# Moving one of three integer additions per score group, and most normalisations, from VectorE to GpSimd

## The chip, the core and the metric

The kernel runs on one core of a Trainium2 chip. The core's engines run side by side, each through its own list of instructions in order: TensorE (PE in the profile) multiplies matrices into PSUM, ScalarE (ACT) applies functions, VectorE (DVE) and GpSimd (POOL) do elementwise work, and SyncE (SP) issues most DMA transfers. An instruction can wait for a semaphore that another engine's instruction raises. The metric is the time of one execution in microseconds (us); lower is better.

## What is computed

Two independent layers share one launch. Part A is attention with 32 query heads and one key and value head. Part B is linear attention, in which queries and keys become two softmaxes of 16 features each.

```python
q = (x @ wq).reshape(B, S, H, Dh)...; k = x @ wk; v = x @ wv          # A: S=2048, H=32, Dh=16
p = softmax(einsum("bhqd,bkd->bhqk", q, k) * Dh**-0.5)
a = einsum("bhqk,bkd->bhqd", p, v)... @ wo
...
phi_k = concat([softmax(k @ w_phi), softmax(-k @ w_phi)])             # B, and phi_q in the same way
kv = einsum("bhsf,bhsd->bhfd", phi_k, v); z = sum over s of phi_k
b = (phi_q @ kv) / (phi_q @ z + 1e-6) @ wo
return concat([a, b], axis=-1)
```

Part A has 32 x 2048 x 2048 exponentials, which is 2048 score tiles of 128 keys by 512 columns. They are most of the work.

## The kernel before, in words

**Two ways to an exponential.** The 2048 score tiles are handled in groups of four (a "quad"): four tiles that share 128 keys and go to one accumulation. 388 of the 512 quads take the ScalarE way. TensorE computes scores in batches of three and two tiles (line 1617, job `qk`), ScalarE exponentiates a batch in one instruction (line 1678, job `ex`, into the ring `PT`), and TensorE multiplies four finished tiles with the values (line 1732, job `pv`, 4 matmuls). The other 124 quads take the VectorE way. TensorE computes one tile at a time (job `dq`, also line 1617), and VectorE turns it into 16-bit integers whose bits, read as a float16, are roughly the exponential (line 1788, job `dz`, into row 0 of the buffer `Z`). When all four tiles of the quad are there, VectorE makes three more versions of them, each the first plus a constant, 256 times 1, 2 and 3 (line 1801, job `dS`, into rows 1 to 3 of `Z`). TensorE then multiplies all four versions with four differently scaled copies of the values and adds them up (line 1834, job `dpv`, 16 matmuls). Their weighted sum is a better exponential than one version alone. `Z` has three buffers (`NQ = 3`).

**After 16 quads** one of the 32 accumulations (`sc`) is complete. VectorE copies it out of PSUM (`ac`, to `accS`), takes the reciprocal of the denominators (`rc`, line 1866), which small DMAs on SyncE gather and spread, and multiplies the two (`on`, line 1884, to `On` or `Od`). The results of eight accumulations feed the output projection of A.

**Part B** is threaded through the first 420 us or so: projections on TensorE, exponentials on ScalarE (lines 2058 and 2148), row sums, reciprocals and products on VectorE. GpSimd sets up constants at the start and does one small step in the middle of B (`kvfin`, lines 2126 to 2131). It does nothing else.

**What sets the order.** A planner in the kernel writes every engine's instruction list ahead of time. Each piece of work is a job with an engine, an assumed duration, a priority and the jobs it needs. The planner keeps a clock for each engine, and always issues the job that can start first by its own assumed durations; among those that could start together the priority decides, with a small random term whose seed changes every 20 us of the plan (`SEEDS`). ScalarE's next score batch has the highest priority on TensorE. The `dq` jobs use what is left of TensorE and VectorE, limited by `dbusy`, an account of VectorE's pending work, so the split between the two ways is an outcome of the plan: a quad that goes to VectorE is one that ScalarE never sees. Where TensorE would otherwise stand idle too long, the planner adds dummy matmuls (`fill` and `company`, lines 1424 and 1407). At run time only semaphores count: each instruction waits for those it depends on, and an engine never goes past a waiting instruction.

Of the kernel before, what the change touches and what calls it, by code (L numbers as in the profile page):

```python
# [7 lines left out]
ALU = mybir.AluOpType  # L8
# [1162 lines left out]
class _Fast:  # L1171
# [16 lines left out]
    def __init__(self, nc, st, ins, out):  # L1188
# [33 lines left out]
        self.ones = sb("ones", [128, 128], BF)  # L1222
        self.zero = sb("zero", [128, 128], BF)
# [41 lines left out]
        self.spq = 30.0  # L1265

# [5 lines left out]
    def add(self, eng, fn, reads=(), writes=(), accum=(), **k):  # L1272
        if self.rec is not None:
            self.rec.append((eng, tuple(reads), tuple(writes) + tuple(accum)))
            return None
        t = self.S.add(eng, fn, reads=reads, writes=writes, accum=accum, **k)
        for r in reads:
            self.tr[r] = max(self.tr.get(r, (0.0, eng)), (self.fin, eng))
# [55 lines left out]
    def issue(self, j, start):  # L1334
# [11 lines left out]
        self.te[j.eng] = max(self.te[j.eng], start + dur)  # L1346
        self.fin = start + dur + self.TAIL[j.eng]
# [90 lines left out]
    def head(self):  # L1438
# [47 lines left out]
        add("pool", lambda g: g.memset(self.bmx, 0.0), writes=["bmx"])  # L1486
        mask = self.mask
# [15 lines left out]
        for k, t in (("wk_rep", 4.5), ("half1", 3.0), ("wv", 5.5), (("wq", 0), 5.0), (("wq", 1), 16.0), (("VA1", 0), 5.0), (("VA1", 1), 12.0), ("odd", 14.0), ("ones", 1.0), ("zero", 1.0), ("bmx", 8.0)):  # L1503
            self.tw[k] = (t, "sp")
# [10 lines left out]
    def jobs_a(self):  # L1515
        ps, xT, job = self.ps, self.xT, self.job
        for kc in range(4):
# [5 lines left out]
            job(("aK", kc), "dve", 0.60, (lambda kc: (lambda: self.absmax(self.KR[:, 0, kc * 512:kc * 512 + 512], kc, [("KR", 0, kc)])))(kc), after=[("KR", 0, kc)], prio=6, rel=30.0 + 5 * kc)  # L1523
# [3 lines left out]
        for ch in range(16):  # L1527
# [4 lines left out]
            job(("aq", ch), "dve", 0.60, (lambda ch: (lambda: self.absmax(self.QA[:, ch % 3, :], 4 + ch, [("QA", ch % 3)])))(ch), after=[("qa", ch)], prio=6, rel=0.0 if ch else 30.0)  # L1532
# [8 lines left out]
        for sc in range(31):  # L1541
            job(("rc", sc), "dve", 0.16, (lambda sc: (lambda: self.finish_sc2(sc)))(sc), after=[("ac", sc)], prio=1.1)
            job(("on", sc), "dve", 0.60, (lambda sc: (lambda: self.finish_sc3(sc)))(sc), prio=1.3,
# [20 lines left out]
    def absmax(self, src, col, reads):  # L1564
        self.add("dve", lambda v: v.tensor_reduce(out=self.mq[:, col:col + 1], in_=src, axis=AX.X, op=ALU.max, apply_absolute_value=True),
# [108 lines left out]
    def expo(self, n0, us, b0):  # L1674
# [5 lines left out]
        if self.rec is None:  # L1680
# [3 lines left out]
            for n in range(n0, n0 + size):  # L1684
                if n % 4 == 3:
                    q = n // 4
                    self.job(("pv", q), "pe", 0.44 if self.aquads[q][0] == 31 else 0.22, (lambda q: (lambda: self.pv(q)))(q), mode="col", prio=1.5,
                             after=[("vb" if self.aquads[q][0] % 2 else "va", self.aquads[q][1] // 4)] + ([("pv", q - 1)] if q else []),
# [764 lines left out]
```

## Time and profile before

| | before |
|---|---|
| median of three runs | 760.16 us (757.96 to 760.37) |
| the profiled execution's own time | 760.35 us |
| its span, first to last instruction | 758.6 us |
| ACT busy | 739.3 us |
| PE busy, of matmuls and their waiting in the pipe | 717.7 us |
| DVE busy | 716.4 us |
| POOL busy | 19.8 us |
| line 1678, exponentials on ScalarE | 621 instructions |
| line 1788, `dz` on VectorE | 496 instructions |
| line 1801, `dS` on VectorE | 372 instructions |
| line 1884, `on` on VectorE | 31 instructions |

The profiled execution took 1.75 us more than its span. The durations of instructions of one engine in the profile overlap each other a little at their ends, so a product of count and mean can be more than the busy time, and the distance from one start to the next is read from a run of equal instructions. A busy TensorE includes the dummy matmuls.

### The profile page before, as it was taken

What the parts mean: (1) busy time and instruction counts of PE and PEld (TensorE: products, weight loads), DVE (VectorE), ACT (ScalarE), POOL (GpSimd) and SP (SyncE); (2) the same over time, 40 slices, a digit from 0 to 9 for tenths busy, and PEclk for the clock granted to TensorE, in tenths of its full rate; (3) what the DMA queues carried; (4) which work ended last, traced back from release to release, by engine and by line L of the source; (5) the groups of instructions that cost most, each with busy time, mean ns of one, the idle gap of its engine ahead of it and who ended that gap; (6) DMA issues with size and microseconds to landing.
All of it is one profiled execution on the core that took longest, in us unless ns stands there. A gap on an engine that the chain in (4) does not pass through costs nothing.

```text
span 758.6 us, 17911 instructions
## 1 busy us (share of the span) xinstructions
PE 717.7 (95%) x7636; PEld 238.7 (31%) x7636; DVE 716.4 (94%) x1249; ACT 739.3 (97%) x692; POOL 19.8 (3%) x73
## 2 busy tenths in 40 slices
PE   8999999999999999999999999999999999999996
PEld 3332333332333223333332223333333333332322
DVE  4999999999999999999999899999999999999981
ACT  5999999999999999999999999999999999999994
POOL 6100000000000000200000000000000000000000
PEclk9999999999999999999999999999999999999999
DMA  9811011110111101111011211111111011111111
GB/s 186 207 10 8 6 9 12 10 8 7 9 12 15 27 8 8 13 10 8 5 9 12 36 23 11 25 19 15 12 23 16 14 35 26 15 26 11 9 9 36
DMA packets 47522, 18.15 MB, mean 24 GB/s; under 512 B 38468, under 2 KB 45572, under 8 KB 47432
## 3 DMA queue, kind: packets, MB, share of 16 engines
q1 hardware_dynamic: 45208, 16.74, 16.5%
q8 instruction: 61, 1.00, 0.5%
q10 hardware_dynamic: 2224, 0.18, 0.2%
q14 instruction: 29, 0.24, 0.1%
HBM read 2.15 MB, written 4.19 MB: 8 GB/s over the span
## 4 chain that ended last, share of the span: by engine, by line
ACT 71%; DVE 15%; PE 12%; DMA 1%; issue 0%; DVEq 0%
ACT f_PT L1678 67%; DVE f_Z L1788 7%; DVE f_Z L1801 5%; PE f_ps L1617 4%; PE f_ps L1834 3%; PE f_ps L1732 2%; ACT f_Ek L2058 2%; ACT f_ET L2148 1%; DMA f_AxT<-in_A_x_dram 1%; PE f_ps L1407 1%; PE f_ps L1923 1%; PE f_ps L1424 1%; DVE f_outA L1430 0%; DVE f_outB L1430 0%; PE f_ps L2141 0%
## 5 line engine op out<-in xcount | busy, mean ns | idle before, releaser
L1678 ACT ACTIVATE f_PT<-f_ps 128x1536 bf16<-128x1536 f32 (+1 forms) x621 | 711.6, 1327 | 9.6 <-PE f_ps L1617 8.9
L1617 PE MATMUL f_ps<-f_QA,f_KR 32*128 32x512 bf16 x2048 | 309.3, 384 | 27.2 <-ACT f_PT L1678 15.2
L1788 DVE TENSOR_SCALAR f_Z<-f_ps 128x512 int16<-128x512 f32 x496 | 322.5, 679 | 11.4 <-PE f_ps L1617 8.4
L1801 DVE TENSOR_SCALAR f_Z<-f_Z 128x2048 int16<-128x2048 int16 x372 | 244.2, 680 | 0.4
L1617 PEld LDWEIGHTS f_ps<-f_QA,f_KR 32*128 32x128 bf16 x2048 | 79.5, 91 | 241.4 <-ACT f_PT L1678 139.7
L1732 PE MATMUL f_ps<-f_PT,f_VA 128*32 128x512 bf16 x1552 | 151.5, 388 | 0.8 <-ACT f_PT L1678 0.2
L1834 PE MATMUL f_ps<-f_Z,f_VK 128*32 128x512 f16 x1984 | 129.7, 381 | 0.9 <-PE f_ps L1732 0.3
L1424 PE MATMUL f_ps<-f_ones,f_zero 128*32 128x512 bf16 (+10 forms) x408 | 69.6, 346 | 2.0 <-POOL f_zero L1442 1.3
L1732 PEld LDWEIGHTS f_ps<-f_PT,f_VA 128*32 128x32 bf16 x1552 | 38.3, 93 | 93.2 <-issue 83.4
L1834 PEld LDWEIGHTS f_ps<-f_Z,f_VK 128*32 128x32 bf16 x1984 | 42.9, 96 | 56.3 <-issue 16.6
L1407 PE MATMUL f_ps<-f_ones,f_zero 32*128 32x512 bf16 x136 | 46.9, 379 | 0.2
L1424 PEld LDWEIGHTS f_ps<-f_ones,f_zero 128*32 128x32 bf16 (+2 forms) x408 | 21.0, 97 | 29.7 <-issue 20.8
L2204 DVE TENSOR_TENSOR f_Wk<-f_ps,f_wq 128x512 bf16<-128x512 f32 x32 | 21.6, 680 | 0.0
L1430 DVE COPY f_accS<-f_ps 128x512 f32<-128x512 f32 x31 | 21.0, 678 | 0.1
L2064 DVE TENSOR_REDUCE f_ssum<-f_Ek 128x64 f32<-128x1024 bf16 x16 | 19.3, 1209 | 0.3 <-ACT f_Ek L2058 0.3
L2090 DVE TENSOR_TENSOR f_vS<-f_ps,f_rs 128x1024 bf16<-128x1024 f32 x16 | 19.5, 1216 | 0.0
L2148 ACT ACTIVATE f_ET<-f_ps 128x512 bf16<-128x512 f32 x32 | 19.1, 710 | 0.0
L2058 ACT ACTIVATE f_Ek<-f_ps 128x512 bf16<-128x512 f32 x32 | 19.1, 709 | 0.0
L1430 DVE CAST f_QA<-f_ps 128x512 bf16<-128x512 f32 x16 | 10.9, 682 | 7.6 <-PE f_ps L1607 7.6
L1607 PE MATMUL f_ps<-f_AxT,f_wq 128*128 128x512 bf16 x64 | 16.6, 381 | 0.8 <-DMA f_AxT<-in_A_x_dram 0.7
L2234 PE MATMUL f_ps<-f_Bwo,f_oT 128*128 128x512 bf16 x64 | 16.6, 382 | 0.1
L2080 PE MATMUL f_ps<-f_Bwv,f_BxT 128*128 128x512 bf16 x64 | 16.6, 381 | 0.1
(100 smaller groups left out, 327.2 us busy)
## 6 DMA issues: line engine op xcount, KB each, us to landing
f_denS<-f_denS SPq DMA_DIRECT2D x124, 30.0 KB, 3.1
out_dram<-f_outB SPq DMA_DIRECT2D x18, 128.0 KB, 2.5
f_denC<-f_accS SPq DMA_DIRECT2D x124, 2.0 KB, 1.7
f_denS<-f_denC SPq DMA_DIRECT2D x124, 2.0 KB, 1.7
out_dram<-f_outA SPq DMA_DIRECT2D x14, 128.0 KB, 1.8
f_On<-f_Od SPq DMA_DIRECT2D x60, 16.0 KB, 1.8
f_Bwv<-in_B_wqkv_dram SPq DMA_DIRECT2D x1, 512.0 KB, 4.9
f_Bwo<-in_B_wo_dram SPq DMA_DIRECT2D x1, 512.0 KB, 5.6
```

The costliest lines, as they stand in the source:

```text
L1407: self.add("pe", lambda pe: pe.matmul(out, lhsT=zero[0:32, :], rhs=rhs, start=False, stop=False, tile_position=(0, 0)), reads=["ones", "ze ...
L1424: mm = pe.matmul(ps[x:x + m, bank, 0:n].rearrange("p (a n) -> p a n", n=128), lhsT=zero[0:r, 0:m], rhs=rhs, start=start, stop=start, **kw)
L1430: self.add("dve", lambda v: v.tensor_copy(out=out, in_=in_), reads=reads, writes=writes)
L1617: return pe.matmul(self.ps[:, bank, :], lhsT=self.KR[32 * g:32 * g + 32, sc % 2, kap * 128:(kap + 1) * 128], rhs=self.QA[32 * g:32 * g + 3 ...
L1678: self.add("act", lambda a: a.activation(out=PT[:, sl[0]:sl[0] + size, :], in_=ps[:, b0:b0 + size, :], func=ACT.Exp), reads=[("PS", b0 + i ...
L1732: mm = pe.matmul(ps[32 * g:32 * g + 32, bank, :], lhsT=w, rhs=PT[:, slots[g], :], start=start, stop=stop, tile_position=(0, 32 * g))
L1788: self.add("dve", lambda v: v.tensor_scalar(out=o, in0=ps[:, bank, :], scalar1=self.Z1, scalar2=self.Z0, op0=ALU.mult, op1=ALU.add), reads ...
L1801: self.add("dve", lambda v: v.tensor_scalar(out=Z[:, t], in0=Z[:, 0], scalar1=256.0 * t, scalar2=None, op0=ALU.add), reads=zk, writes=[("Z ...
L1834: mm = pe.matmul(ps[32 * g:32 * g + 32, bank, :], lhsT=w[:, k, :], rhs=Zf[:, k, sl[g], :], start=start and k == 0, stop=stop and k == 3, t ...
L2058: self.add("act", (lambda a, sg: (lambda e: e.activation(out=Ek[:, r, a].rearrange("p h f -> p (h f)"), in_=ps[:, bank, :], func=ACT.Exp, ...
L2148: self.add("act", lambda e: e.activation(out=self.ET[:, sl, :], in_=self.ps[:, bank, :], func=ACT.Exp, scale=sg), reads=[("PS", bank)], wr ...
L2204: self.add("dve", lambda v: v.tensor_tensor(out=o, in0=i, in1=w.unsqueeze(3).to_broadcast([128, 16, 2, 16]), op=ALU.mult), reads=[("PS", b ...
```

## The change

1. **The third shift goes to GpSimd.** `PSH = 4` tiles, that is the whole of row 3 of `Z`, are no longer made by VectorE. A job `dP` on GpSimd adds to row 0, read as 32-bit integers, the constant 768 x 65537, which adds 768 to both 16-bit halves at once: 1024 elements in each partition in place of 2048. The constant is one column, `step3`, which is read for every element. The planner assumes `PDUR = 2.0` us for it. `dP` reads what the quad's other two shifts wrote as well, so it starts after both.
2. **28 of the 31 normalisations `on` go to GpSimd** (`ONP = 28`, with an assumed 1.35 us); the last three stay on VectorE.
3. [...] In the plan, no shift or `on` of VectorE overlaps with work of GpSimd: `port` holds the end of the other engine's last such job, and such jobs start after it. At run time, GpSimd's `dP` and `on` also wait for the last VectorE job of these kinds that was planned ahead of them (`last_lock`). VectorE gets no wait for GpSimd from this.
4. `dbusy` counts two pending shifts per quad, and the seeds of the order are others. The jobs `aK`, `aq`, `ss` and `pv` get options whose values leave them as they were.

```diff
+        self.step3 = sb("step3", [128, 1], I32)
+        self.port = dict(dve=0.0, pool=0.0)
+        self.last_lock = None
...
     def add(self, eng, fn, reads=(), writes=(), accum=(), **k):
+        lock = k.pop("lock", False)
+        if lock and eng == "pool" and self.last_lock is not None:
+            k["deps"] = [self.last_lock]
         t = self.S.add(eng, fn, reads=reads, writes=writes, accum=accum, **k)
+        if lock and eng == "dve":
+            self.last_lock = t
...
+        if j.name[0] in self.PAIR or j.eng == "pool":
+            self.port[j.eng] = start + dur
...
+        add("pool", lambda g: g.memset(self.step3, 768 * 65537), writes=["step3"])
...
-            job(("on", sc), "dve", 0.60, ...
+            job(("on", sc), "pool" if sc < self.ONP else "dve", self.ODUR if sc < self.ONP else 0.60, ...
...
-                self.dbusy += 1.2 if h == 3 else -0.6
+                self.dbusy += 1.2 - 0.15 * self.PSH if h == 3 else -0.6
...
-        def shift(t):
+        def shift(eng, t, a, b):
             def go():
-                self.add("dve", lambda v: v.tensor_scalar(out=Z[:, t], in0=Z[:, 0], scalar1=256.0 * t, scalar2=None, op0=ALU.add),
-                         reads=zk, writes=[("Zt", p, t)])
-                if self.rec is None:
-                    self.dbusy -= 0.6
+                if eng == "pool":
+                    w = lambda x: Z[:, x, a:b].bitcast(I32).rearrange("p a n -> p (a n)")
+                    self.add("pool", lambda g: g.tensor_tensor(out=w(t), in0=w(0), in1=self.step3.to_broadcast([128, 256 * (b - a)]), op=ALU.add),
+                             reads=zk + ["step3"] + [("Zt", p, x, "dve") for x in (1, 2)], writes=[("Zt", p, t, eng)], lock=True)
+                    return
+                self.add(eng, lambda v: v.tensor_scalar(out=Z[:, t, a:b], in0=Z[:, 0, a:b], scalar1=256.0 * t, scalar2=None, op0=ALU.add),
+                         reads=zk, writes=[("Zt", p, t, eng)], lock=True)
+                if self.rec is None and eng == "dve":
+                    self.dbusy -= 0.15 * (b - a)
             return go
+        aft = []
         for t in range(1, 4):
-            self.job(("dS", quad, t), "dve", 0.60, shift(t), after=[("dz", k - x) for x in range(4)], prio=2)
-        aft = [("dS", quad, t) for t in range(1, 4)]
+            n = 4 - self.PSH if t == 3 else 4
+            if n:
+                aft.append(("dS", quad, t))
+                self.job(aft[-1], "dve", 0.07 + 0.133 * n, shift("dve", t, 0, n), after=[("dz", k - x) for x in range(4)], prio=2)
+            if n < 4:
+                self.job(("dP", quad), "pool", self.PDUR, shift("pool", t, n, 4), after=list(aft), prio=2)
+                aft.append(("dP", quad))
...
-        self.add("dve", lambda v: v.tensor_tensor(out=o, in0=accS[:, r, :], in1=R[:, r, :], op=ALU.mult),
-                 reads=[("accS", r), ("denS", r), ("row", r)], writes=[key])
+        self.add("pool" if sc < self.ONP else "dve", lambda v: v.tensor_tensor(out=o, in0=accS[:, r, :], in1=R[:, r, :], op=ALU.mult),
+                 reads=[("accS", r), ("denS", r), ("row", r)], writes=[key], lock=True)
...
+    AENG, ADUR, SENG, SDUR, ONP, ODUR = 'dve', 0.6, 'dve', 1.13, 28, 1.35
+    PSH = 4
+    PDUR = 2.0
+    PAIR = ("dS", "on", "dP")
...
                     r = self.ready(j)
+                    if r is not None and (j.name[0] in self.PAIR or j.eng == "pool"):
+                        r = max(r, self.port["dve" if eng == "pool" else "pool"])
```

What this does to the written-out lists, counted over the whole program:

| instructions | before | after |
|---|---|---|
| score tiles exponentiated on ScalarE (in 621, then 610 instructions) | 1552 | 1524 |
| quads on the VectorE way | 124 | 131 |
| `dz` on VectorE | 496 | 524 |
| `dS` on VectorE | 372 | 262 |
| `on` on VectorE | 31 | 3 |
| `dP` on GpSimd | 0 | 131 |
| `on` on GpSimd | 0 | 28 |
| matmuls of `pv` (line 1732, 1748 after) on values and for denominators | 1600 | 1572 |
| matmuls of `dpv` (line 1834, 1861 after) on values and for denominators | 2048 | 2160 |
| dummy matmul instructions (`fill` and `company`) | 544 | 447 |

The 610 instructions are 305 of three tiles, 304 of two and one of one; the 621 before are 310 of three and 311 of two. Lines have moved by some 10 to 30 in the changed file.

VectorE, about 60% into the list, before: four `dz` of a quad (line 1788), the shifts (line 1801) and copies out of PSUM for other jobs (line 1430).

```order
L1788 TENSOR_SCALAR f_Z<-f_ps 128x512 [waits s_pe] x4
L1801 TENSOR_SCALAR f_Z<-f_Z 128x2048 [waits s_dve]
L1801 TENSOR_SCALAR f_Z<-f_Z 128x2048
L1430 COPY f_outA<-f_ps 128x512 [waits s_pe,d_out3]
L1788 TENSOR_SCALAR f_Z<-f_ps 128x512 [waits s_pe]
L1801 TENSOR_SCALAR f_Z<-f_Z 128x2048
```

The same engine after, about 70% into its shorter list (`dz` is line 1804, `dS` line 1822):

```order
L1804 TENSOR_SCALAR f_Z<-f_ps 128x512 [waits s_pe] x2
L1822 TENSOR_SCALAR f_Z<-f_Z 128x2048 [waits s_dve]
L1804 TENSOR_SCALAR f_Z<-f_ps 128x512 [waits s_pe] x2
L1822 TENSOR_SCALAR f_Z<-f_Z 128x2048
L1440 COPY f_oT<-f_ps 128x512 [waits s_pe]
```

A quad has two shifts left on VectorE, and they stand apart, among other work.

GpSimd after, over several quads; before, its list has nothing between the set-up and `kvfin`. `dP` is line 1819, `on` line 1911.

```order
L1819 TENSOR_TENSOR f_Z<-f_Z,f_step3 128x1024 [waits s_pool,s_dve] x3
L1911 TENSOR_TENSOR f_On<-f_accS,f_denS 128x512 [waits s_pool,d_dma7]
L1819 TENSOR_TENSOR f_Z<-f_Z,f_step3 128x1024 [waits s_pool,s_dve] x4
L1819 TENSOR_TENSOR f_Z<-f_Z,f_step3 128x1024 [waits s_pool]
L1911 TENSOR_TENSOR f_Od<-f_accS,f_denS 128x512 [waits s_pool,d_dma10]
```

Every addition waits for the GpSimd instruction ahead of it, and most for VectorE too; an `on` waits for a DMA (`d_dma`), and the additions queue behind it.

TensorE before, at a `dpv` (line 1834) between two score batches:

```order
L1617 MATMUL f_ps<-f_QA,f_KR 128x512 [waits s_act]
L1617 MATMUL f_ps<-f_QA,f_KR 128x512 x2
L1834 MATMUL f_ps<-f_Z,f_VK 32x512 [waits s_dve]
L1834 MATMUL f_ps<-f_Z,f_VK 32x512 x15
L1617 MATMUL f_ps<-f_QA,f_KR 128x512 [waits s_act]
```

and after (scores are line 1628, `dpv` line 1861):

```order
L1628 MATMUL f_ps<-f_QA,f_KR 128x512 [waits s_act]
L1628 MATMUL f_ps<-f_QA,f_KR 128x512 x2
L1861 MATMUL f_ps<-f_Z,f_VK 32x512 [waits s_pool]
L1861 MATMUL f_ps<-f_Z,f_VK 32x512 x15
L1628 MATMUL f_ps<-f_QA,f_KR 128x512 [waits s_act]
```

The 16 matmuls of a VectorE quad now wait for GpSimd, and ScalarE's next score batch stands behind them on TensorE.

37 lines of the change are left out of this document (22 added, 15 removed).

## The prediction

> **What bounds the kernel now.** I read the page's table of busy time first, then the table of stretches, then the chain, since a high share of the span can mean a limit or only an even load.
>
> ```profile
> PE 717.7 (95%) x7636; PEld 238.7 (31%) x7636; DVE 716.4 (94%) x1249; ACT 739.3 (97%) x692; POOL 19.8 (3%) x73
> ACT 71%; DVE 15%; PE 12%; DMA 1%; issue 0%; DVEq 0%
> ```
>
> ```profile
> 0.00:20.00 20.00, 17.40 (x139) 6.67 (x143) 8.80 (x26) 11.41 (x10) 13.20 (x58) 1.00 1.00 190
> 110.00:160.00 50.00, 48.37 (x543) 16.57 (x543) 49.78 (x87) 50.00 (x51) 0.00 (x0) 1.00 0.11 8
> 460.00:510.00 50.00, 47.85 (x500) 16.06 (x498) 49.74 (x86) 50.00 (x45) 0.00 (x0) 1.00 0.14 19
> 745.00:758.60 13.60, 6.61 (x48) 2.08 (x44) 2.26 (x4) 4.51 (x8) 0.00 (x0) 0.91 0.13 43
> ```
>
> The columns after the stretch are its length and the busy time of PE, weight loads, DVE, ACT and POOL. In both middle stretches, one with part B and one without, ScalarE is busy for all of the 50 us. ScalarE is idle only at the start (8.6 us of the first 20) and at the end (9.1 us of the last 13.6), together 17.7 of its 19.3 idle us. VectorE is as full, but the chain goes over ScalarE for 71% of the span. So time is what ScalarE has to do, plus a start and an end that the change leaves as they are. The other engines matter where they make ScalarE wait, or where they limit how many quads can be taken off it.
>
> **ScalarE's load.**
>
> ```profile
> L1678 ACT ACTIVATE f_PT<-f_ps 128x1536 bf16<-128x1536 f32 x310 | 476.7, 1540 | 8.6 <-PE f_ps L1617 8.0
> L1678 ACT ACTIVATE f_PT<-f_ps 128x1024 bf16<-128x1024 f32 x311 | 345.4, 1114 | 1.0 <-PE f_ps L1617 1.0
> ```
>
> ```profile
> 459.64 71.70 ACT f_PT L1678 x63
> ```
>
> A score tile of 512 columns more costs 1540 - 1114 = 426 ns. The longest unbroken piece of the chain has 63 instructions in 71.70 us, 1.138 us each, or 2.276 us for a pair of three and two tiles; less 5 x 0.426 that leaves 0.146, so 0.073 us for each instruction's start. The order after has 28 tiles fewer and 11 instructions fewer: 28 x 0.426 + 11 x 0.073 = 11.9 + 0.8 = 12.7 us less. Nothing is added to ScalarE. From the profiled execution's own 760.35 us (0.19 above the median of the runs) that leaves 747.6, if ScalarE stays as full as it is.
>
> **VectorE's load.**
>
> ```profile
> L1788 DVE TENSOR_SCALAR f_Z<-f_ps 128x512 int16<-128x512 f32 x496 | 322.5, 679 | 11.4 <-PE f_ps L1617 8.4
> L1801 DVE TENSOR_SCALAR f_Z<-f_Z 128x2048 int16<-128x2048 int16 x372 | 244.2, 680 | 0.4
> ...
> L1884 DVE TENSOR_TENSOR f_On<-f_accS,f_denS 128x512 bf16<-128x512 f32 x16 | 10.8, 676 | 2.2 <-DMA f_denS<-f_denS 2.2
> ```
>
> ```profile
> 738.10 1.90 DVE L1801 TENSOR_SCALAR f_Z<-f_Z 128x2048 int16<-128x2048 int16 x3
> ```
>
> One of these takes 0.68 us by its record, but three in a row take 1.90, so the next starts (1.90 - 0.68) / 2 = 0.61 us after the last. VectorE loses 110 shifts and 28 products and gains 28 `dz`: (110 + 28 - 28) x 0.61 = 67 us off 716. It is no longer nearly full; it has about 67 + 42 = 109 us to spare in which delays can be made good.
>
> **TensorE's load.**
>
> ```profile
> L1732 PE MATMUL f_ps<-f_PT,f_VA 128*32 128x512 bf16 x1552 | 151.5, 388 | 0.8 <-ACT f_PT L1678 0.2
> L1834 PE MATMUL f_ps<-f_Z,f_VK 128*32 128x512 f16 x1984 | 129.7, 381 | 0.9 <-PE f_ps L1732 0.3
> L1424 PE MATMUL f_ps<-f_ones,f_zero 128*32 128x512 bf16 (+10 forms) x408 | 69.6, 346 | 2.0 <-POOL f_zero L1442 1.3
> ...
> L1407 PE MATMUL f_ps<-f_ones,f_zero 32*128 32x512 bf16 x136 | 46.9, 379 | 0.2
> ```
>
> By busy time per instruction, 112 more matmuls of `dpv` add 112 x 129.7 / 1984 = 7.3 us, and 28 fewer of `pv` remove 28 x 151.5 / 1552 = 2.7. The 97 dummies that go are worth 97 x (69.6 + 46.9) / 544 = 21. TensorE has no more to do than before, so I add nothing for it. The granted clock, 1.00 in the middle stretches, I take to stay there: real matmuls take the place of dummies.
>
> **The new addition.** The trace has no 32-bit addition. GpSimd's nearest rows are its two-input products in part B and its copies:
>
> ```profile
> L1595 POOL COPY f_VK<-f_VK 128x64 bf16<-128x64 bf16 x16 | 4.4, 272 | 2.4 <-DVE f_VK L1587 0.5
> L2126 POOL TENSOR_TENSOR f_KVn<-f_kvS,f_mask 128x128 bf16<-128x128 f32 x8 | 4.3, 534 | 286.1 <-DVE f_kvS L2117 285.5
> ...
> L1476 POOL COPY f_wk_rep<-f_wk_raw 128x512 bf16<-128x512 bf16 x1 | 0.6, 612 | 0.9 <-DMA f_wk_raw<-in_A_wk_dram 0.9
> ...
> L2131 POOL TENSOR_TENSOR f_KVs<-f_kvS,f_mask 128x64 bf16<-128x64 f32 x1 | 0.3, 318 | 0.1
> ```
>
> ```profile
> L2126 POOL TENSOR_TENSOR f_KVn<-f_kvS,f_mask x8: 403/404/772, 315.9 to 320.4; 128x128 bf16<-128x128 f32 x8
> ```
>
> ```profile
> L1801 DVE TENSOR_SCALAR f_Z<-f_Z x372: 622/681/892, 26.5 to 739.3; 128x2048 int16<-128x2048 int16 x186
> ```
>
> ```profile
> 315.77 0.68 DVE L1884 TENSOR_TENSOR f_Od<-f_accS,f_denS 128x512 bf16<-128x512 f32 x1
> 316.37 0.89 DVE L1801 TENSOR_SCALAR f_Z<-f_Z 128x2048 int16<-128x2048 int16 x1
> ```
>
> ```profile
> 315.94 0.77 POOL L2126 TENSOR_TENSOR f_KVn<-f_kvS,f_mask 128x128 bf16<-128x128 f32 x1 [285.55 <-DVE f_kvS L2117]
> ```
>
> Lower bound, one input: the copies cost (612 - 272) / 448 = 0.76 ns per column, so 1024 columns take 0.61 + 512 x 0.76 ns = 1.0 us. Undisturbed, the two-input product takes 404 ns for 128 columns and 318 for 64: 1.34 ns per column, and 404 ns + 896 x 1.34 ns = 1.6 us for 1024. Upper bound, with the mean of 534 ns, which includes collisions: 3.4 ns per column, 3.6 us. I take 1.6 to 2.0 us, near the second, since it is the same kind of instruction without disturbance; the additions' plain rows of 1024 are no harder than the short strided runs of line 2126.
>
> Where does this time lie? VectorE has two shifts of the quad done, and its list goes on; nobody but TensorE waits for the addition. In the written-out order, 59 of the 131 `dpv` stand no more than five score tiles of ScalarE behind the place of their addition, and half stand seven or more behind: five tiles are 5 x 1.138 / 2.5 = 2.3 us. An addition of up to 2.2 us ends in time, and the sum gets 0 for it. Behind a `dpv` that waits stands the next score batch, and then ScalarE. TensorE has this to give before ScalarE notices:
>
> ```profile
> PEld f_ps L1617 <- ACT f_PT L1678: 139.7, 357, 0.9
> ...
> ACT f_PT L1678 <- PE f_ps L1617: 8.9, 4, 7.8
> ...
> PEld f_ps L1834 <- DVE f_Z L1801: 7.3, 27, 0.4
> ```
>
> Score batches waited for ScalarE 357 times, 0.39 us each, and ScalarE waited for scores only 4 times, once for 7.8 us at the start. So a `dpv` late by up to about 0.4 us costs little, and a later one costs what is over.
>
> [...]
>
> **The shared port.** The rows at 315.8 us show what an overlap does. The GpSimd product that began beside VectorE's two-input product took 772 ns in place of 404, and the shift that began while it ran took 892 in place of 681. So each can hold the other up, by 0.2 to 0.4 us there, and by up to a whole addition with longer ones. The plan keeps shifts and `on` apart from GpSimd's work; it does not keep apart these VectorE instructions in part B, whose operands are in on-chip memory like those:
>
> ```profile
> L1430 DVE CAST f_vS<-f_rs 128x64 bf16<-128x64 f32 x16 | 4.9, 306 | 0.0
> ...
> L2070 DVE TENSOR_TENSOR f_bmx<-f_ssum,f_bmx 128x64 f32<-128x64 f32 x16 | 3.3, 209 | 0.0
> ...
> L2182 DVE TENSOR_TENSOR f_wq<-f_wq,f_rden 128x256 f32<-128x256 f32 x4 | 1.7, 413 | 0.0
> L2178 DVE TENSOR_TENSOR f_rden<-f_sden 128x128 f32<-128x128 f32 x4 | 1.1, 282 | 0.0
> ```
>
> That is 40 instructions. GpSimd works for about 131 x 1.8 + 28 x 1.1 = 267 of 745 us, 0.36 of the time, and one that meets it waits half an addition, 0.9 us: 40 x 0.36 x 0.9 = 13 us of VectorE time. VectorE's spare 109 us absorbs most; I let 3 us reach ScalarE, between 0 and 13.
>
> The `on` jobs take 1.1 us by the same rate, 0.5 longer than on VectorE, and `dP` jobs queue behind one that waits for its DMA. Line 1884 waited for a DMA for 2.2 us in all before, so I take 0, with up to 28 x 0.2 = 6 us as the bad end. The four DMAs behind an odd `on` on SyncE start later by as much; what reads them comes an accumulation later, some 23 us.
>
> **The end.** Before, ScalarE waits once there:
>
> ```profile
> 745.19 1.94 ACT L1678 ACTIVATE f_PT<-f_ps 128x1024 bf16<-128x1024 f32 x2 [0.75 <-PE f_ps L1617]
> ```
>
> Two batches of two tiles are the last; after, it is one tile, with as many matmuls of the output behind it. Between -0.75 and +1 us; I take 0.
>
> **Sum:** 760.35 - 12.7 + 3 = 750.6, which I round to 750.5.
>
> **Rivals.**
>
> *The addition is late (slower).* If the mean of 534 ns is the true cost, the addition takes 3.6 us, is late by 1.3 us at 59 `dpv`, and after 0.4 of slack costs 59 x 0.9 = 53 us: 801 us. It decides from the point where 59 x (late - 0.4) is 12.7, a lateness of 0.6 and an addition of 2.8 us. A moderate 3.0 us gives 747.6 + 59 x 0.3 = 765. For it: every `dpv` now has this wait, and TensorE goes past none. Against it: the median of the eight products is 404 ns, and the slow ones lie beside VectorE work of the kinds that the plan now keeps apart.
>
> *Waits at the port give the gain back.* If each of the 131 additions also holds one of VectorE's shifts for half its length, 131 x 0.9 = 118 us use up all of the 109 us that VectorE has to spare, and VectorE is again as full as before. The change then does not do what it says: 757 to 764, about 760. For it: the 892 ns shift; at run time VectorE does not wait for GpSimd by a semaphore. Against it: the plan separates them, and a shift is one of many VectorE jobs that can stand there.
>
> *More gain.* The 7.3 us that `dpv` waited for shifts, and waits of scores for VectorE, get shorter with a freer VectorE, and the clashes cost nothing: 747.6 - 3 = 744.6.
>
> **How the numbers follow.** I give my forecast 0.66, the late addition 0.16, the port 0.13 and more gain 0.05. A measurement of this kernel tells 0.3% from no change, so faster means below 757.9 and slower above 762.5. Of the port's 0.13, 0.04 falls on faster, 0.06 on the same, 0.03 on slower. Faster is 0.66 + 0.05 + 0.04 = 0.75, the same 0.06, slower 0.16 + 0.03 = 0.19. The forecast's own range is 746 to 757. For 8 in 10 I leave out most of the late addition above 768 (0.12) and the best of the gains below 745 (0.04): 745 to 768.
>
> **What would show it.** Right: line 1678 with 610 instructions and about 12.7 us less in the chain, ScalarE still full in the middle stretches, the addition's median at 1.6 to 2.0 us, VectorE at 650 us busy, and weight loads of line 1861 that hardly wait for GpSimd. Wrong: weight loads of line 1861 that wait for line 1819 by tens of us and score batches for which ScalarE waits in the middle (late addition); or shifts on line 1822 with a mean far above 680 ns and a VectorE busy as before (port). I would be wrong, too, if the clock fell below 1.00 with fewer dummies.

## The result

The changed kernel takes 750.39 us (median of 4 runs, 749.14 to 751.64) against 760.26 us for the kernel before on the same chip (4 runs, 757.96 to 760.94): a ratio of 0.9875 with a 95% interval of 0.9849 to 0.9902. It is 1.2% faster. The profiled execution took 750.23 us, with a span of 748.5.

The page after, busy time and chain:

```profile
PE 711.2 (95%) x7623; PEld 236.4 (32%) x7623; DVE 670.6 (90%) x1139; ACT 728.7 (97%) x681; POOL 301.9 (40%) x233
ACT 63%; PE 20%; DVE 14%; DMA 1%; issue 1%; POOL 0%; SPq 0%; DVEq 0%
```

The chain still lies mostly on ScalarE, but 8 points of it have gone over to TensorE. The same two middle stretches as in the prediction (busy us of PE, weight loads, DVE, ACT and POOL):

```profile
110.00:160.00 50.00, 47.34 (x560) 15.26 (x552) 48.80 (x85) 49.74 (x46) 19.56 (x11) 1.00 0.11 9
460.00:510.00 50.00, 47.84 (x540) 16.26 (x533) 46.71 (x81) 49.72 (x45) 20.41 (x12) 1.00 0.15 17
```

ScalarE was busy for 50.00 of 50 us before, and for 49.7 now: it loses some 0.3 us in each stretch. The granted clock is still 1.00. VectorE has 1 to 3 us free in each stretch, though GpSimd does 20 us of work there.

The groups by line and shape (count, busy us and mean ns, then the idle time before them and what ended it):

```profile
L1689 ACT ACTIVATE f_PT<-f_ps 128x1536 bf16<-128x1536 f32 x305 | 462.7, 1517 | 10.0 <-PE f_ps L1628 9.4
...
L1689 ACT ACTIVATE f_PT<-f_ps 128x1024 bf16<-128x1024 f32 x304 | 330.7, 1091 | 1.9 <-PE f_ps L1628 1.0
...
L1819 POOL TENSOR_TENSOR f_Z<-f_Z,f_step 128x1024 int32<-128x1024 int32 x131 | 247.8, 1892 | 387.1 <-DVE f_Z L1822 385.7
...
L1822 DVE TENSOR_SCALAR f_Z<-f_Z 128x2048 int16<-128x2048 int16 x262 | 176.2, 697 | 2.0 <-POOL f_Z L1819 1.4
...
L1440 DVE CAST f_vS<-f_rs 128x64 bf16<-128x64 f32 x16 | 7.0, 437 | 0.0
...
L2097 DVE TENSOR_TENSOR f_bmx<-f_ssum,f_bmx 128x64 f32<-128x64 f32 x16 | 5.0, 315 | 0.1
```

An addition takes 1892 ns. GpSimd is idle for 386 us ahead of its additions, until a shift of VectorE ends. That is not the price of the wait that the change added at run time: without it (`e3_no_port_wait` below) these idle times come to 405 us, so the additions wait above all for their quad's own shifts. The shifts' mean rose from 680 to 697 ns, the casts' from 306 to 437, and the `bmx` products' from 209 to 315.

**Where the time went.** ScalarE's usual step, from the end of one exponential to the end of the next, has a median of 1.343 us for three tiles, 0.917 for two and 0.490 for one tile or a step of part B, the same before and after. The sum of these steps is what ScalarE needs; what its exponentials took beyond that sum, I call lost. The four short ones of 256 columns behind the last score batch count to the end. The span then has four parts:

| us | start, to the end of the first exponential | needed | lost | end, after the last exponential |
|---|---|---|---|---|
| before | 11.32 | 731.53 | 4.27 | 11.50 |
| after | 11.04 | 718.89 | 8.96 | 9.61 |
| difference | -0.28 | -12.64 | +4.69 | -1.89 |

The smaller load is there in full, and 4.7 us of it were given back as time that ScalarE lost. The end does not look like a gain of the change: a run of the same order in the experiments had 11.63 us there, another 9.33, and the difference lies behind the issue of the last output transfer, which landed 3.95 us after it before and 1.83 us after. Each of these four parts comes from one profiled execution, so whether the changed kernel has the short end more often stays open.

### The profile page after: what moved, and what is told of

Read it like the earlier page. It is cut to its first block, busy times and chain, and to the rows that moved or that the text cites. A ratio compares the mean times of both kernels' runs of the same rounds, so it can differ in the third digit from the quotient of the medians.

```text
span 748.5 us, 18063 instructions
## 1 busy us (share of the span) xinstructions
PE 711.2 (95%) x7623; PEld 236.4 (32%) x7623; DVE 670.6 (90%) x1139; ACT 728.7 (97%) x681; POOL 301.9 (40%) x233
## 4 chain that ended last, share of the span: by engine, by line
ACT 63%; PE 20%; DVE 14%; DMA 1%; issue 1%; POOL 0%; SPq 0%; DVEq 0%
ACT f_PT L1689 60%; PE f_ps L1628 7%; DVE f_Z L1804 5%; PE f_ps L1748 4%; PE f_ps L1861 4%; DVE f_Z L1822 3%; ACT f_ET L2175 2%; DVE f_vS L2117 1%; ACT f_Ek L2085 1%; PE f_ps L1417 1%; PE f_ps L1618 1%; PE f_ps L1434 1%; DVE f_ssum L2091 1%; DMA f_AxT<-in_A_x_dram 1%; PE f_ps L1950 1%
## 5 line engine op out<-in xcount | busy, mean ns | idle before, releaser
L1689 ACT ACTIVATE f_PT<-f_ps 128x1536 bf16<-128x1536 f32 (+1 forms) x610 | 699.9, 1303 | 11.9 <-PE f_ps L1628 10.4
L1819 POOL TENSOR_TENSOR f_Z<-f_Z,f_step 128x1024 int32<-128x1024 int32 x131 | 247.8, 1892 | 387.1 <-DVE f_Z L1822 385.7
L1804 DVE TENSOR_SCALAR f_Z<-f_ps 128x512 int16<-128x512 f32 x524 | 340.6, 681 | 28.9 <-PE f_ps L1628 23.2
L1822 DVE TENSOR_SCALAR f_Z<-f_Z 128x2048 int16<-128x2048 int16 x262 | 176.2, 697 | 2.0 <-POOL f_Z L1819 1.4
L1748 PE MATMUL f_ps<-f_PT,f_VA 128*32 128x512 bf16 x1524 | 148.0, 388 | 0.8 <-DVE f_accS L1440 0.2
L1861 PE MATMUL f_ps<-f_Z,f_VK 128*32 128x512 f16 x2096 | 137.0, 381 | 1.1 <-PE f_ps L1748 0.8
L1434 PE MATMUL f_ps<-f_ones,f_zero 128*32 128x512 bf16 (+11 forms) x317 | 57.3, 351 | 1.5 <-POOL f_zero L1452 1.3
L1911 POOL TENSOR_TENSOR f_Od<-f_accS,f_denS 128x512 bf16<-128x512 f32 x14 | 17.8, 1269 | 18.2 <-DVE f_Z L1822 17.2
L1434 PEld LDWEIGHTS f_ps<-f_ones,f_zero 128*32 128x32 bf16 (+2 forms) x317 | 17.2, 97 | 23.5 <-issue 17.0
L1911 POOL TENSOR_TENSOR f_On<-f_accS,f_denS 128x512 bf16<-128x512 f32 x14 | 17.8, 1273 | 14.7 <-DVE f_Z L1822 13.7
```

The costliest lines, as they stand in the source:

```text
L1434: mm = pe.matmul(ps[x:x + m, bank, 0:n].rearrange("p (a n) -> p a n", n=128), lhsT=zero[0:r, 0:m], rhs=rhs, start=start, stop=start, **kw)
L1689: self.add("act", lambda a: a.activation(out=PT[:, sl[0]:sl[0] + size, :], in_=ps[:, b0:b0 + size, :], func=ACT.Exp), reads=[("PS", b0 + i ...
L1748: mm = pe.matmul(ps[32 * g:32 * g + 32, bank, :], lhsT=w, rhs=PT[:, slots[g], :], start=start, stop=stop, tile_position=(0, 32 * g))
L1804: self.add("dve", lambda v: v.tensor_scalar(out=o, in0=ps[:, bank, :], scalar1=self.Z1, scalar2=self.Z0, op0=ALU.mult, op1=ALU.add), reads ...
L1819: self.add("pool", lambda g: g.tensor_tensor(out=w(t), in0=w(0), in1=self.step3.to_broadcast([128, 256 * (b - a)]), op=ALU.add), reads=zk ...
L1822: self.add(eng, lambda v: v.tensor_scalar(out=Z[:, t, a:b], in0=Z[:, 0, a:b], scalar1=256.0 * t, scalar2=None, op0=ALU.add), reads=zk, wri ...
```

## Experiments

All times are medians beside runs of the kernel before on the same chip. "Needed", "lost" and "held" are of the one profiled execution, whose own time can lie off the median: 748.13 us in `e2`, 810.59 in `e4`, 797.26 in `e10`, 767.79 in `e6`. "Held" is VectorE time: the sum over its instructions of what they took above the usual duration of their kind, where that is over 0.09 us. All but `e5` to `e8` and `e11` have the changed kernel's order of work word for word, so what ScalarE needs is equal in them.

| run | median us | ratio to before, 95% | needed | lost | held |
|---|---|---|---|---|---|
| before | 760.26 | | 731.53 | 4.27 | 0.2 |
| after | 750.39 | 0.9875 (0.9849 to 0.9902) | 718.89 | 8.96 | 7.8 |
| e1_control | 750.73 | 0.9869 (0.9833 to 0.9905) | 718.89 | 8.91 | 7.8 |
| e2_short_pool | 750.33 | 0.9862 (0.9821 to 0.9902) | 718.89 | 6.84 | 0.7 |
| e3_no_port_wait | 758.82 | 0.9977 (0.9951 to 1.0002) | 718.89 | 17.97 | 19.2 |
| e4_late_1us | 803.40 | 1.054 (1.0487 to 1.0593) | 718.89 | 67.50 | 47.0 |
| e9_hold_same | 764.42 | 1.0049 (1.0006 to 1.0092) | 718.89 | 22.28 | 32.2 |
| e10_late_only | 800.22 | 1.0552 (1.0509 to 1.0595) | 718.89 | 54.15 | 19.9 |
| e6_plain_none | 765.32 | 1.0077 (1.0054 to 1.0099) | 733.37 | 9.13 | 0.4 |
| e7_plain_both | 764.37 | 1.0048 (1.0019 to 1.0077) | 722.49 | 16.82 | 15.8 |
| e8_plain_cap | 776.47 | 1.0206 (1.0156 to 1.0255) | 733.37 | 20.75 | 14.7 |
| e11_plain_both_dummies | 765.99 | 1.0086 (1.0053 to 1.0118) | 724.33 | 16.04 | 14 |
| e5_hold_after | 778.94 | 1.0246 (1.0195 to 1.0298) | 729.70 | 23.92 | 32.0 |

My theory was that the gain is ScalarE's smaller load less a few us of clashes between VectorE and GpSimd. The rivals were the late addition and clashes that give the gain back. "Port" is my name for what the two clash at; the runs show which instructions were held and for how long, not a port.

**e1_control** is the changed kernel again.

> The changed kernel as it stands, as the control for the runs beside it. About 750.4 us, ratio to the kernel before 0.9875; ScalarE's time lost between its first and last exponential about 9 us, against 4.3 us before, in its profile.

It repeats the result, with the same 19 VectorE instructions held, by the same 7.8 us in all.

**e2_short_pool** leaves the order as it is and makes GpSimd's instructions short, the additions from the fourth quad on and the `on` from accumulation 12 on; the rest of those rows is not computed.

```diff
+                    c = 1024 if quad < 3 else 32
-                    w = lambda x: Z[:, x, a:b].bitcast(I32).rearrange("p a n -> p (a n)")
-                    self.add("pool", lambda g: g.tensor_tensor(out=w(t), in0=w(0), in1=self.step3.to_broadcast([128, 256 * (b - a)]), op=ALU.add),
+                    w = lambda x: Z[:, x, a:b].bitcast(I32).rearrange("p a n -> p (a n)")[:, 0:c]
+                    self.add("pool", lambda g: g.tensor_tensor(out=w(t), in0=w(0), in1=self.step3.to_broadcast([128, c]), op=ALU.add),
...
+        n = 32 if 12 <= sc < self.ONP else 512
-        self.add("pool" if sc < self.ONP else "dve", lambda v: v.tensor_tensor(out=o, in0=accS[:, r, :], in1=R[:, r, :], op=ALU.mult),
+        self.add("pool" if sc < self.ONP else "dve", lambda v: v.tensor_tensor(out=o[:, 0:n], in0=accS[:, r, 0:n], in1=R[:, r, 0:n], op=ALU.mult),
```

> Same written-out order on every engine; from the fourth group on, GpSimd adds only 32 of the 1024 columns, and multiplies only 32 of the 512 columns from accumulation 12 on, so the rest of those rows is left uncomputed. GpSimd's instructions become short (estimate 0.35 us in place of 1.89 and 1.27). Theory 'port': what ScalarE loses over the kernel before (4.7 us) comes from VectorE instructions held up by GpSimd, so nearly all 19 stretched VectorE instructions go and the time falls by 3 to 5 us, to 746 or 747. Theory 'TensorE': the loss comes from score batches that end late behind other matmuls in this order, whatever GpSimd does, so the time stays within 1 us of the control, about 750. Theory 'late additions': as 'port', 3 to 5 us less, but with the gain at places where the 16 matmuls of a VectorE group waited for GpSimd.

The page of this run:

```profile
PE 711.0 (95%) x7623; PEld 236.4 (32%) x7623; DVE 663.3 (89%) x1139; ACT 728.0 (98%) x681; POOL 74.2 (10%) x233
ACT 79%; PE 14%; DVE 5%; DMA 0%; issue 0%; SPq 0%; DVEq 0%; POOL 0%; POOLq 0%
```

GpSimd's work falls from 302 to 74 us, VectorE is held by 0.7 us in place of 7.8, and the chain is back on ScalarE. ScalarE still loses 6.84 us: 2.1 of the 4.7 us given back went away, and the median time does not differ from the control's by more than the runs spread, as I had written down for the theory 'TensorE'. So by the trace, clashes of VectorE with GpSimd and the addition's length explain less than half of what was given back. The other 2.6 us stay when GpSimd hardly works, so they belong to the order of work, not to GpSimd. In the trace they look like tight fits on TensorE. One of them, after (TensorE, then ScalarE, start and length in us), and ScalarE at the same place in e2:

```profile
588.82 0.87 PE L1748 MATMUL f_ps<-f_PT,f_VA 128*32 128x512 bf16 x8
589.63 1.04 PE L1618 MATMUL f_ps<-f_AxT,f_wq 128*128 128x512 bf16 x4
590.60 0.39 PE L1628 MATMUL f_ps<-f_QA,f_KR 32*128 32x512 bf16 x3
```

```profile
591.03 2.37 ACT L1689 ACTIVATE f_PT<-f_ps 128x1024 bf16<-128x1024 f32 x2 [0.32 <-PE f_ps L1628]
```

```profile
589.67 3.28 ACT L1689 ACTIVATE f_PT<-f_ps 128x1024 bf16<-128x1024 f32 x3 [0.32 <-PE f_ps L1628]
```

The score batch at 590.60 stands behind twelve other matmuls, and ScalarE waits 0.32 us for it, with long additions and with short ones. After the first score batch ScalarE waits more than 0.15 us for scores at eight places; at six of these e2 has the wait too, at five of them as long to 3 ns. Losses of this size are spread over the span (in the changed kernel 0.3 to 1.3 us in each 50 us after the first). That such fits are the 2.6 us is read from the trace and was not tried by itself.

**e3_no_port_wait** takes away the run-time wait of GpSimd for VectorE's last planned shift. The additions keep their own wait for the shifts of their quad.

```diff
-        if lock and eng == "pool" and self.last_lock is not None:
-            k["deps"] = [self.last_lock]
```

> Same written-out order; GpSimd's additions and products no longer wait for the last VectorE shift of another group, only for what they read. Theory 'the wait matters at run time': GpSimd starts some instructions beside a VectorE shift and is held up or holds it up, so shifts over 0.8 us become more than the 7 of now and the time rises by 1 to 5 us. Theory 'the plan alone keeps them apart': starts differ by under 0.2 us, the time stays within 1 us of the control.

It costs 8 us, where I had written 1 to 5: with the wait gone, the gain over the kernel before can no longer be told from nothing. One of the holds (VectorE, then GpSimd):

```profile
73.85 2.98 DVE L1820 TENSOR_SCALAR f_Z<-f_Z 128x2048 int16<-128x2048 int16 x2
```

```profile
74.01 2.27 POOL L1817 TENSOR_TENSOR f_Z<-f_Z,f_step 128x1024 int32<-128x1024 int32 x1 [1.32 <-DVE f_Z L1820]
```

Two shifts in a row take 0.61 + 0.68 = 1.29 us otherwise. Here the addition begins during the first, takes 2.27 us in place of 1.89, and the second shift is held for 1.7 us. VectorE is held by 11.4 us more than in the control, and ScalarE loses 9.1 us more. VectorE was busy for 680.9 of 757.8 us in this run, so it had 77 us free in all, and these did not absorb the holds. The chain of its page lies on VectorE for 25% of the span, where the changed kernel's has 14%. I read this so: behind a held shift stands the next `dz`, which decides when a PSUM tile is free for TensorE's next scores.

**e4_late_1us** puts a clearing of the addition's own target row ahead of each addition, which takes 951 ns.

```diff
+                    self.add("pool", lambda g: g.memset(w(t), 0), reads=zk + [("Zt", p, x, "dve") for x in (1, 2)], writes=[("Zt", p, t, eng)], lock=True)
```

> Same written-out order; a clearing of the same 1024 columns (0.96 us on GpSimd for as many in the kernel before) stands ahead of every addition, so that each third version is there about 1.0 us later. Working of the prediction: 59 groups have only 2.3 us, the addition then ends at 2.9 us, TensorE gives 0.4: 59 x 0.2 = 12 us slower than the control, 762. If the slack of TensorE is smaller than 0.4 us, up to 59 x 0.6 = 35 us, 785. If groups make up for each other, because an addition that is late finds TensorE waiting at other places anyway, under 6 us, below 756.

The waits of this run (us in all, times, longest; line 1862 is `dpv`, 1820 the addition):

```profile
ACT f_PT L1689 <- PE f_ps L1628: 55.7, 83, 7.4
...
PEld f_ps L1862 <- POOL f_Z L1820: 44.1, 59, 2.2
...
PE f_ps L1862 <- POOL f_Z L1820: 24.9, 44, 1.7
```

It is 53 us slower than the control, where I had forecast some 12, at most 35. The weight loads of `dpv` waited 44 us for additions, against 2.6 us in the changed kernel; the waits of its matmuls on the third line lie within these. But VectorE was also held by 47 us, since the clearings collide with shifts, so this run alone does not tell lateness from holding.

**e5_hold_after** was to add only the holding: a clearing of a scratch tile behind each addition, which no one waits for. The planner took notice of the new tile, and the order came out with 125 quads on the VectorE way in place of 131.

```diff
+        self.scr = sb("scr", [128, 896], F32)
...
+                    self.add("pool", lambda g: g.memset(self.scr, 0.0), writes=["scr"])
```

> Same written-out order; a clearing of a scratch tile (896 32-bit columns, 0.85 us by the rate of the 0.96 us for 1024) stands behind every addition in place of ahead of it. The third version is on time, but GpSimd is at work about 0.9 us longer after each. Theory 'late for the matmuls' (the 53 us of the 1 us delay came from TensorE waiting for the addition): under 8 us slower than the control, below 759. Theory 'held VectorE' (most of them came from VectorE instructions held up for 47 us in that run in place of 8): VectorE held up for 20 to 45 us, and 20 to 45 us slower than the control, 770 to 796. Since a clearing only writes, a third way is that it holds up shifts but not two-input instructions.

10.8 us of its 778.94 are ScalarE's larger load, so it answers nothing by itself. **e9_hold_same** is the same with the clearing hidden from the planner, and **e10_late_only** is to add lateness: seven clearings of one column behind each addition, 128 ns each, for whose last the `dpv` waits.

```diff
+                    if self.rec is None:
+                        self.S.add("pool", lambda g: g.memset(self.scr, 0.0), writes=["scr"])
```

> Same written-out order as the changed kernel, 131 groups (the earlier run with the clearing behind the addition came out with 125 groups, so it was not that). The clearing of a scratch tile, 0.85 us, stands behind every addition; the matmuls wait for the addition alone. Theory 'held VectorE': with VectorE held up for 25 to 35 us in place of 8, ScalarE loses 15 to 30 us more than the control's 8.9, 765 to 780. Theory 'late for the matmuls': under 8 us slower, below 759.

```diff
+        self.scr = sb("scr", [128, 1], F32)
...
+                    if self.rec is None:
+                        for _ in range(7):
+                            self.S.add("pool", lambda g: g.memset(self.scr, 0.0), writes=["scr", ("Zt", p, t, eng)])
```

> Same written-out order. Behind every addition stand seven clearings of a single column, about 0.14 us each by the rows of such clearings before, and the 16 matmuls wait for the last: they get their third version about 1.0 us later, while GpSimd hardly uses the port in that time. In the control 43 of 131 groups have under 1.0 us between the addition's end and their matmuls, together 18 us of lateness. Theory 'late for the matmuls': ScalarE loses at most these 18 us, plus what TensorE's pauses cost in clock, 760 to 775. Theory 'held VectorE': within 3 us of the control. The 53 us of the 1 us delay should be about the sum of this and the run with the clearing behind.

The waits of the two runs, e9 first (in each, line 1820 is the addition, the line of `f_scr` the clearing):

```profile
ACT f_PT L1690 <- PE f_ps L1629: 19.6, 25, 7.9
...
PEld f_ps L1864 <- POOL f_Z L1820: 6.3, 15, 1.3
...
PEld f_ps L1864 <- POOL f_scr L1823: 3.9, 12, 0.4
```

```profile
PEld f_ps L1865 <- POOL f_scr L1824: 57.4, 66, 2.6
...
ACT f_PT L1690 <- PE f_ps L1629: 48.1, 69, 7.6
...
PE f_ps L1865 <- POOL f_scr L1824: 36.0, 45, 2.3
```

In e9 VectorE is held by 24 us more than in the control, ScalarE loses 13.4 us more, and the time rises by 13.7 us, to just under the range that I had given for the holds. In e10 VectorE is held by 12 us more, the weight loads of `dpv` wait 57 us for the last clearing, ScalarE loses 45 us more, and the time rises by 49.5 us. 13.4 + 45.2 is 58.6 us, what ScalarE loses more in e4.

Neither run is pure. In e9 the weight loads of `dpv` wait 10 us for GpSimd in place of 2.6, and of e10's 45 us some 7 go with its 12 us of holds, by e9's rate of 13.4 to 24 (an estimate). Even so both rivals were real mechanisms, and lateness is the dearer by far: of 131 additions in the control only 43 end less than 1 us ahead of their `dpv`, and the sum of what these would lack is 18 us, yet a delay of about that 1 us (the last clearing ends 1.10 us after the addition, by the median) costs some 50, outside what either theory had given e10. The chain of its page no longer lies on ScalarE, but goes round the other three engines:

```profile
DVE 37%; PE 29%; POOL 20%; ACT 7%; issue 4%; SPq 1%; DMA 1%; DVEq 0%; POOLq 0%
```

I read this so: the `dpv` that waits holds up the scores behind it, also those of the next `dq`, so the next quad's `dz`, shifts and addition are late as well, and the plan's gaps do not come back within a quad. That this loop multiplies the delay was not tried by itself.

**e6 to e8 and e11: the order without its seeds.** Without the small random term in the priorities (all seeds 0) the same code can be planned with neither move (`e6`: `PSH = 0, ONP = 0`), with both (`e7`), and with both but no more than the 123 quads of e6 (`e8`, the only one with the last two lines below, and with `CAP = 123`).

```diff
-    SEEDS = (993870, 533796, 241805, 467285, 693828, 478729, 0, 780962, 791015, 164751, 32308, 775891, 917256,
...
+    SEEDS = (0,)
...
+        if len(self.dquads) >= self.CAP:
+            return None
```

> The changed kernel's planner with no random term in the priorities (all seeds zero), and with shifts and products all on VectorE. 123 groups on VectorE in this order. A baseline for the next two. Its order was not selected, so ScalarE loses more than in the kernel before: about 5 us for that and 1.8 for one group fewer, 767.

> As the baseline without random term, but with the third shift and 28 products on GpSimd as in the change: 129 groups on VectorE, so 24 tiles fewer on ScalarE than in the baseline: 24 x 0.426 + 10 x 0.073 = 11 us less if the offload is what pays, 756. If the changed kernel's gain came from its other seeds, within 3 us of the baseline.

> As the run with both moves and no random term, but VectorE takes no more than 123 groups, as many as the baseline. Theory 'only ScalarE's tile count pays': within 2 us of the baseline, 767, though VectorE has some 60 us less to do. Theory 'a freer VectorE pays by itself' (TensorE and ScalarE wait less for it): half or more of the gain stays, 761 or less.

The pages of e6, e7 and e8, busy time:

```profile
PE 725.5 (95%) x7659; PEld 239.8 (31%) x7659; DVE 713.3 (93%) x1242; ACT 743.0 (97%) x694; POOL 19.3 (3%) x74
```

```profile
PE 722.4 (95%) x7680; PEld 239.2 (31%) x7680; DVE 667.8 (88%) x1127; ACT 733.1 (96%) x684; POOL 299.0 (39%) x231
```

```profile
PE 730.9 (94%) x7672; PEld 240.4 (31%) x7672; DVE 644.8 (83%) x1091; ACT 744.4 (96%) x694; POOL 287.4 (37%) x225
```

From e6 to e7 the VectorE way takes 129 quads in place of 123, ScalarE needs 10.9 us less, and loses 7.7 us more: the medians are 765.32 and 764.37. That is what I had written down beforehand for a gain that came from the other seeds (within 3 us), not for the offload (756): without the seeds the smaller load is there, the gain hardly. From e6 to e8 ScalarE's load is the same, VectorE has 68.5 us less to do, and the kernel is 11 us slower. So in these orders a freer VectorE does not pay for what the moves cost. The changed kernel's gain comes from the quads that ScalarE is spared, and how much of it is kept depends on the order. Of the 7.9 us that ScalarE loses more in e7 than in the changed kernel, 4.9 also stand between e6 and the kernel before, where GpSimd does no additions. The rest goes along with more holds (15.8 us of VectorE time against 7.8); that shifts and additions meet more rarely in the searched order is not shown to be its cause.

**e11_plain_both_dummies** is e7 with more dummy matmuls, since e7 showed stretches of half clock (its mean granted clock was 0.993, and 0.90 from 197 to 204 us).

```diff
-    ACTIVE = 4.5
-    FORCE = 3.3
+    ACTIVE = 5.5
+    FORCE = 3.8
```

> As the run with both moves and no random term, but the planner adds dummy matmuls below an activity of 5.5 and 3.8 in place of 4.5 and 3.3. 128 groups in place of 129, 1.8 us more for ScalarE. Theory 'clock': ScalarE lost 5.1 us there around the stretches of half clock; with none of these the run gains about 5 - 1.8 = 3 us, 761. Theory 'VectorE's waits': the half clock is a sign of pauses and costs nothing of its own, the time rises by 2 us or more for the group and the dummies, 766 or above.

The half clock was gone from its profile but for the end (a mean of 0.999), and it was no faster than e7 (765.99 against 764.37 us): TensorE was busy for 733.8 us in place of 722.4, and ScalarE needs 1.8 us more in the order that came out.

## Why the prediction was right, and where it was not

The prediction was 750.5 us, the measurement 750.39. The forecast's mechanism is the one that the runs show: ScalarE is spared 28 tiles and gives a little of it back. That the number met the measurement to 0.1 us is luck: two of its terms were off and made up for each other.

- **ScalarE's load, -12.7 us.** Measured -12.64.
- **Port clashes in part B, +3 us.** ScalarE lost 4.7 us more. I had 13 us of VectorE time on 40 instructions of part B. It was 3.7 us on 7 of them (3 `bmx`, 4 casts), and 4.0 us on 12 shifts, which I had taken as kept apart by the plan: they are apart in the plan's durations, and at run time no semaphore makes VectorE wait for GpSimd's additions and `on`. By e2, clashes and the additions' length are 2.1 of the 4.7 us; the other 2.6, the looser fit of the new order, had no term in my sum.
- **The end and the start, 0.** They were 2.2 us shorter in the profiled run, which hid that the loss was larger than forecast. They are not a part of the change's effect, as far as the runs tell.
- **"VectorE's spare 109 us absorbs most."** This step failed as reasoning. VectorE was busy for 670.6 us, not 650, so 78 us were free: 7.8 us more are holds, and its instructions overlap at their ends by 77 us in all in place of 95, since they follow each other directly less often, so that taking one out saves less than I had counted. And what it has free does not absorb holds: of 11.4 us more held in e3, ScalarE lost 9.1, of 24.3 in e9, 13.4. The small sum came out because few instructions were held.
- **TensorE no more to do, the clock at 1.00.** 711.2 us after 717.7, and 1.00 in the middle stretches.
- **The addition, 1.6 to 2.0 us.** It took 1.890 to 1.897 us, 131 times. `on` took 1.27 us where I had 1.1 "by the same rate"; the rate of 1.34 ns for each column would have given 0.92.
- **`dpv` hardly waits for GpSimd.** Its weight loads waited 2.6 us in all, in 8 waits of at most 0.4: what I took as free.
- **The rival of the late addition** named the right place and a price that was far too low. An addition's end at 1.89 + 1.10 = 3.0 us was to cost 59 x 0.3 = 18 us; in e10 it cost 49.5. The slack of 0.4 us, counted anew for each use, is what I think was wrong: one delay uses it up for the next. I had the gain gone at an addition of 2.8 us (2.9 with the 2.3 us of the rest of that sum), 0.9 longer than it is. By proportion from e10, an estimate, 1.10 x 9.9 / 49.5 = 0.2 us longer would do; a small delay may cost less than its proportion, which no run tried.
- **The rival at the port** is what happens without the added wait (e3), though by another way than the one I described: VectorE did not get full again, it was late at the wrong moments. I had not costed that wait at all. It is worth 8 us, most of the gain.
- **The order.** I took the counts of the written-out order as given and did not ask whether another order would do as well. With the plain one, the same moves bring a time that is hardly better than with neither. A run of the searched kind with the moves left out, in the changed planner, is missing; the kernel before is the nearest to it.

## What to carry to other kernels

An engine's idle share is not slack: in a chain of in-order queues, 1.1 us of delay at work that is used just in time cost 50 us here, where the margins that it overran lacked 18 us, and time free elsewhere did not pay it back. Before moving work to a slower engine, list how long ahead of its use each result is ready, and price the uses with less than a microsecond as if each delayed everything behind it. If two engines hold each other up, let the one with time to spare wait for the other by a semaphore; here that wait is worth 8 of 10 us. And compare in more than one order of work, or the order's own share of a gain stays hidden.

## What the runs showed of the hardware

**Where VectorE and GpSimd clashed, the instruction that began first kept its time.** In the changed kernel all 19 holds are VectorE instructions that began while GpSimd was at an addition (13) or at an `on` (6), and GpSimd's took their usual 1.89 and 1.27 us. One of them (VectorE, then GpSimd):

```profile
394.33 0.68 DVE L1804 TENSOR_SCALAR f_Z<-f_ps 128x512 int16<-128x512 f32 x1
394.93 2.00 DVE L1822 TENSOR_SCALAR f_Z<-f_Z 128x2048 int16<-128x2048 int16 x1
```

```profile
394.49 1.89 POOL L1819 TENSOR_TENSOR f_Z<-f_Z,f_step 128x1024 int32<-128x1024 int32 x1 [6.54 <-DVE f_Z L1822]
```

The `dz`, whose input is in PSUM, runs beside the addition at its usual 0.68 us, like the 147 `dz` that lie within an addition or an `on` (0.62 to 0.69 us). The shift, whose input is in on-chip memory, begins 0.44 us after the addition and ends 0.55 us after its end, 1.3 us late; the addition is not lengthened. All 19 held instructions ended after the GpSimd instruction beside which they began: the 12 shifts 0.55 us after it, the 4 casts 0.17 to 0.18, the 3 `bmx` 0.08. It goes the other way too: in e3 20 additions began 0.16 us after a shift and took 2.27 us in place of 1.89. A clearing by GpSimd, which reads nothing, holds shifts too: in e9 30 shifts began during a clearing, ended 0.55 us after it, and were held by 12.1 us in all. Two `bmx` products, which read two inputs, began during a clearing as well and took their usual 0.21 us.

**In e3 the granted clock fell to a half at two places, at one of them with TensorE nearly always busy just before.** They are at 170.8 and 269.8 us, and the clock is 0.50 for the 3.40 us read at each. The stretches before and at each (same columns as above, the granted clock behind the POOL column):

```profile
168.00:170.80 2.80, 0.93 (x8) 0.26 (x6) 2.77 (x5) 1.90 (x2) 2.52 (x2) 1.00 0.26 11
...
170.80:174.20 3.40, 3.40 (x30) 0.74 (x26) 2.93 (x5) 1.65 (x2) 0.24 (x1) 0.50 0.06 15
...
266.00:268.00 2.00, 1.93 (x17) 0.49 (x15) 1.97 (x3) 2.00 (x3) 1.49 (x1) 1.00 0.21 14
268.00:269.80 1.80, 1.60 (x15) 0.37 (x13) 1.80 (x4) 1.80 (x2) 0.40 (x1) 0.99 0.57 35
...
269.80:273.20 3.40, 3.40 (x28) 0.77 (x32) 2.37 (x4) 1.78 (x3) 0.85 (x1) 0.50 0.21 9
```

The first follows a stretch of 2.80 us with TensorE idle for 1.87 of them, the second a stretch with TensorE busy for 3.5 of 3.8 us, but with 8 matmuls a microsecond where the middle stretches have 11. What brings the clock down, no run shows by itself. The kernels before and after and e2 have no half clock ahead of their ends (mean granted clocks of 0.998, 1.000 and 1.000). The runs' mean granted clocks suggest a price: over 45 runs of the kernel before, the time lies on a line of 758.4 us at full clock and 0.33 us more for each us at half clock (correlation 0.93); 12 runs of e3 give 756.4 and 0.46, 10 runs of e7 759.3 and 0.43. That is a correlation and not a trial, and the end has a part in it: in the profile of the kernel before, all half clock lies from 756.25 us on (0.50 over the last 2.35 us), behind the last matmul, while the last output transfer is under way, so there a late landing makes both the time and the half clock longer. By these lines the changed kernel stands at 749.9 at full clock (10 runs), 8.5 us ahead of the kernel before, close to the 12.64 - 4.69 = 7.95 us that ScalarE's own account gives. They fit e11 as well: its runs were at a clock of 0.998 and it took 766, while e7's line reaches 759.3 at full clock, so the added dummies, with the 1.8 us more that ScalarE needs there, cost about as much as the half clock that they removed.
